# Transposing part of the softmax weights with VectorE and DMA instead of TensorE, in an attention and feed-forward kernel

## The chip, the cores and the metric

The kernel runs on one core of one Trainium2 chip. The metric is the device time in microseconds (us) of one execution. Of the kernel before there are three runs: 1382.41, 1383.41 and 1386.02 us, median 1383.41 us.

## The reference

Attention over 4 batches of 8 heads, with queries averaged in neighbouring pairs, followed by two feed-forward layers.

```python
batch, n_heads, seq, head_dim = (4, 8, 1152, 64)
q_pool = q.reshape(B, H, S // 2, 2, D).mean(axis=3)          # 576 queries per head
scores = scale * np.matmul(q_pool, k.transpose(0, 1, 3, 2))
scores = scores - np.max(scores, axis=-1, keepdims=True)
attn = np.exp(scores)
attn = attn / (np.sum(attn, axis=-1, keepdims=True) + 1e-09)
x = np.matmul(attn, v)                       # heads side by side: (2304, 512)
h = x @ w_in;  x = np.maximum(0.01 * h, h) @ w_out            # d_ff 2048
h = x @ w_in2; out = np.where(h > 0, h, np.exp(np.minimum(h, 0)) - 1) @ w_out2
```

All inputs are float32 except the four weight matrices, which arrive as float64.

## The kernel before

Precision. TensorE works on a reduced float32 type (F32R). Every operand that matters is split in two: a high part, rounded to F32R by a copy, and a low part, which is the value less the high part. `psplit` (L342) emits the two: the copy, mostly on ScalarE ("ACT"), and the subtraction on VectorE ("DVE") or GpSimd ("POOL"). The weights arrive as float64, and `convert` (L356) turns them into float32 bit by bit on ScalarE, VectorE and GpSimd.

Attention. A head pair (`attn_pair`, L631) is two heads of a batch; there are 16, in order. For each head the keys are transposed to `kT`, the queries summed in pairs, transposed and split to `qT`, the values split to `vn`. A pair has nine query tiles of 128 rows: four per head, and a ninth that holds the last 64 queries of both heads. For each tile `scores` (L517) works in three thirds of 384 keys: two matmuls per third into a PSUM bank (L531), the maximum on VectorE (L536, L538), and the exponential on ScalarE (L542), which leaves the third of P, the unnormalised softmax weights, as `p` in SBUF, with queries in partitions and keys along the row. P times V needs the keys in partitions, so `transpose_p` (L548) lets TensorE transpose three 128x128 blocks per third into a PSUM bank (L554), ScalarE copies the bank to the high part of `pt` (L345) and VectorE subtracts for the low part (L352). `pt` is one buffer per third for a group of two tiles (256 queries; 320 where the ninth tile joins). `pv` (L568) runs six matmuls per third and group (L578), then adds the two partial results into `xu` (L592).

Feed-forward. `mlp` (L676) runs a layer for one batch: for each of 16 slices of 128 hidden columns an up-projection (L721) with its activation and split, and for every four slices a down-projection (L755). `load_w` (L390) brings a slice's weights: the first time it loads, converts and splits them and writes both parts to DRAM; afterwards it loads the split parts, two transfers of 256 KB per matrix and slice, one for each part.

Order. Nothing runs in the order of the code. Every operation is entered with `prog.add` under an engine, a cost in nanoseconds and a rank; `Program.schedule` (L101) plays the program through with these costs and, whenever an engine is free, starts the ready operation of the lowest rank. `LATENCY` gives the delay from the end of an operation to its users; `HOLD`, `GAP`, `PATIENCE` and the bank caps are its further rules. The order so found is the order in each engine's queue. A pair has nine ranks; `PLAN` gives each batch and layer of the feed-forward its first rank and its span, so that its matmuls fill TensorE beside the attention of later pairs. All DMAs are issued by SyncE ("SP"), in one queue in that order, and wait there for their data. Buffers of a tag are used in rotation: an operation that first writes a buffer waits for the readers of the one `bufs` places before.

## Time and profile before

| | |
|---|---|
| profiled execution, whole | 1383.44 us |
| its span, first to last instruction | 1381.6 us |
| TensorE busy | 1346.1 us (97%) |
| ScalarE, VectorE, GpSimd busy | 903.0, 833.0, 523.7 us |
| DMA engines, mean share of the hardware queue | 43.5% |
| chain that ended last: TensorE, ScalarE, VectorE | 72%, 13%, 8% |

Times are microseconds from the span's start unless marked ns. "PE" is TensorE's matmul unit, "PEld" its weight load, which runs beside it. A matmul's busy time overlaps that of its neighbours, so the pace of TensorE is read from one start to the next and not from durations. The DMA share is the mean busy share of the core's 16 DMA engines. The time splits into three stages: to about 535 us the first nine pairs run beside the conversion of the weights and, later in it, the first feed-forward layers; from 535 to 1100 us the last seven pairs run beside the feed-forward of batches 1 and 2; after 1100 us only batch 3's feed-forward is left.

### The profile page before, as it was taken

The page shows a single profiled execution, that of the slowest core. Times are in us where ns is not written, and L with a number is a line of the kernel's source. Part 1 is how long each engine was busy: PE and PEld are TensorE (multiplying, and loading weights), DVE is VectorE, ACT ScalarE, POOL GpSimd, SP SyncE. Part 2 cuts the span into 40 slices and gives each one's busy share as a digit, 9 for nine tenths or more (in the row PEclk, how much of TensorE's full clock was granted, in tenths as well). Part 3 has the DMA queues.
Part 4 walks back from the last instruction along what each step waited for, and adds up shares of the span by engine and source line. Part 5 has one row for each costly group of instructions (what it writes and reads, how often), then busy time and mean ns, then how long its engine had stood idle before and what let it go on. Part 6 is the DMA issues. An engine that isn't in the chain of part 4 may idle for free.

```text
span 1381.6 us, 22560 instructions
## 1 busy us (share of the span) xinstructions
PE 1346.1 (97%) x7664; PEld 1161.1 (84%) x7664; DVE 833.0 (60%) x1919; ACT 903.0 (65%) x2391; POOL 523.7 (38%) x492
## 2 busy tenths in 40 slices
PE   7998999999999999999999999999999999999998
PEld 6887888888788888888888888888888888888887
DVE  6899997888888975455555555556555421232122
ACT  8999999898999976654666666564665333214331
POOL 4334466677767742221313132131311222223221
PEclk9999999999999999999999999999999999999999
DMA  4323446656566565433333444343443343333321
GB/s 139 113 88 98 156 146 211 217 197 212 188 215 219 192 214 169 144 132 131 116 119 129 137 164 147 122 164 115 147 137 139 136 168 122 123 107 137 122 77 46
DMA packets 119475, 202.29 MB, mean 146 GB/s; under 512 B 12608, under 2 KB 31040, under 8 KB 119360
## 3 DMA queue, kind: packets, MB, share of 16 engines
q1 hardware_dynamic: 119360, 200.85, 43.5%
q8 instruction: 61, 1.00, 0.3%
q14 instruction: 54, 0.44, 0.1%
HBM read 162.53 MB, written 38.27 MB: 145 GB/s over the span
## 4 chain that ended last, share of the span: by engine, by line
PE 72%; ACT 13%; DVE 8%; DMA 3%; POOL 2%; issue 2%; SPq 0%; ACTq 0%; POOLq 0%
PE b L755 26%; PE b L721 24%; PE b L578 7%; PE b L531 7%; PE b L554 6%; ACT p L542 4%; ACT pt L345 3%; DVE m L536 2%; DMA cr<-in_moe_w_out_dram 2%; DVE pt L352 2%; ACT cm L375 1%; ACT ct L377 1%; DVE wr L384 1%; PE b L485 1%; PE b L457 1%
## 5 line engine op out<-in xcount | busy, mean ns | idle before, releaser
L721 PE MATMUL b<-xs,wi 128*128 128x512 f32 x1440 | 404.0, 402 | 2.5 <-POOL xs L352 0.8
L721 PEld LDWEIGHTS b<-xs,wi 128*128 128x128 f32 x1440 | 256.2, 189 | 47.2 <-ACT p L542 1.1
L352 DVE TENSOR_TENSOR pt<-b,pt 128x384 fp32r<-128x384 f32 (+1 forms) x480 | 233.7, 511 | 90.4 <-ACT pt L345 87.5
L352 POOL TENSOR_TENSOR g<-t,g 128x512 fp32r<-128x512 f32 x112 | 144.8, 1294 | 364.6 <-ACT g L345 257.4
L542 ACT ACTIVATE p<-b,m 128x384 f32<-128x384 f32 x432 | 253.3, 600 | 24.8 <-DVE m L538 24.0
L345 ACT ACTIVATE pt<-b 128x384 fp32r<-128x384 f32 (+1 forms) x480 | 208.1, 470 | 82.0 <-PE b L554 81.0
L536 DVE TENSOR_REDUCE m<-b 128x1 f32<-128x384 f32 x432 | 230.3, 550 | 51.6 <-PE b L531 47.3
L554 PE MATMUL b<-ident,p 128*128 128x128 f32 x1296 | 200.3, 274 | 5.8 <-DVE pt L352 1.4
L755 PE MATMUL b<-g,wo 128*128 128x512 f32 x696 | 200.7, 403 | 0.0
L755 PE MATMUL b<-wo,g 128*128 128x512 f32 x696 | 198.8, 403 | 0.7 <-DVE t L739 0.7
L531 PE MATMUL b<-kT,qT 128*128 128x384 f32 x768 | 192.6, 352 | 5.5 <-DVE pt L352 2.6
L554 PEld LDWEIGHTS b<-ident,p 128*128 128x128 f32 x1296 | 159.9, 141 | 42.8 <-DVE pt L352 4.0
L578 PE MATMUL b<-pt,vn 128*128 128x256 f32 (+1 forms) x1152 | 191.0, 300 | 3.7 <-DVE pt L352 1.7
L578 PEld LDWEIGHTS b<-pt,vn 128*128 128x128 f32 x1152 | 169.4, 188 | 17.7 <-DVE pt L352 6.2
L531 PEld LDWEIGHTS b<-kT,qT 128*128 128x128 f32 x768 | 131.8, 191 | 21.3 <-DVE pt L352 3.5
L755 PEld LDWEIGHTS b<-wo,g 128*128 128x128 f32 x696 | 123.3, 188 | 20.5 <-DVE t L739 1.2
L755 PEld LDWEIGHTS b<-g,wo 128*128 128x128 f32 x696 | 121.9, 188 | 17.1
L382 POOL TENSOR_TENSOR wr<-wr,ct 128x256 uint32<-128x256 uint32 x128 | 92.4, 737 | 58.1 <-DVE wr L379 26.3
L769 DVE TENSOR_TENSOR acc<-b,acc 128x512 f32<-128x512 f32 x96 | 65.9, 687 | 72.3 <-PE b L755 71.0
L345 ACT ACTIVATE g<-t 128x512 fp32r<-128x512 f32 x112 | 71.2, 638 | 42.0 <-DVE t L732 24.9
L730 ACT ACTIVATE t<-b 128x512 f32<-128x512 f32 (+1 forms) x65 | 37.6, 584 | 93.1 <-PE b L721 92.1
L732 DVE TENSOR_TENSOR t<-b,t 128x512 f32<-128x512 f32 (+1 forms) x65 | 43.0, 663 | 89.7 <-ACT t L730 89.4
(117 smaller groups left out, 1694.5 us busy)
## 6 DMA issues: line engine op xcount, KB each, us to landing
wi<-w SPq DMA_DIRECT2D x176, 256.0 KB, 3.7
wo<-w SPq DMA_DIRECT2D x176, 256.0 KB, 3.8
cr<-in_moe_w_in_dram SPq DMA_DIRECT2D x64, 256.0 KB, 2.8
cr<-in_moe_w_out_dram SPq DMA_DIRECT2D x64, 256.0 KB, 3.2
w<-wi SPq DMA_DIRECT2D x64, 256.0 KB, 3.4
w<-wo SPq DMA_DIRECT2D x64, 256.0 KB, 3.4
raw<-in_k_dram SPq DMA_DIRECT2D x32, 288.0 KB, 3.7
raw<-in_v_dram SPq DMA_DIRECT2D x32, 288.0 KB, 3.4
```

The lines of the kernel that those rows point to most:

```text
L345: prog.add("ACT", act(n, sbuf=not psum), rank, lambda: A.activation(out=hi(), in_=src(), func=ACTF.Copy), w=[w], r=r)
L352: lambda: eng.tensor_tensor(out=lo(), in0=src(), in1=f32(hi()), op=ALU.subtract),
L382: prog.add("POOL", pool(CW), rank, lambda t=t, to=to: G.tensor_tensor(out=to(), in0=to(), in1=t.ap, op=ALU.add), w=part, r=[t] + part)
L531: PE.matmul(out=st[:, 0:384], lhsT=qa(a), rhs=kT[:, 384 * c:384 * c + 384], start=(i == 0), stop=(i == len(seq) - 1))
L536: prog.add("DVE", dve(384), rank - LR, lambda st=st, c=c: V.tensor_reduce(out=m[:, c:c + 1], in_=st[:, 0:384], axis=AX.X, op=ALU.max), w=[ ...
L542: prog.add("ACT", act(384, True), rank - LE, lambda c=c: A.activation(out=p[c].ap, in_=banks[c][:, 0:384], func=ACTF.Exp, bias=m[:, 3:4], ...
L554: PE.transpose(out=t[:, i, :], in_=p[c][:, 128 * i:128 * i + 128], identity=ident)
L578: PE.matmul(out=o[:, 0:n], lhsT=vn[:, c, :], rhs=pt[th][:, a, c % 3, :], start=(c == 3 * ORDER[0] and a == 0), stop=(c == 3 * ORDER[2] + 2 ...
L721: PE.matmul(out=h[:, 0:n], lhsT=wi[:, a, c, :], rhs=xs[hf][c][:, e], start=(c == 0 and a == 0 and e == 0), stop=(c == DC - 1 and a == 1))
L732: prog.add("DVE", dve(n), rk, lambda tn=tn, hn=hn: V.tensor_tensor(out=tn(), in0=hn(), in1=tn(), op=ALU.max), w=[t], r=[h, t])
L755: PE.matmul(out=y[:, 0:n], lhsT=g[f][hf][:, e, part] if layer else w[f][1][:, a, part], rhs=w[f][1][:, a] if layer else g[f][hf][:, e], st ...
L769: prog.add("DVE", dve(n), rank - HURRY, lambda y=y, a_=a_, n=n: V.tensor_tensor(out=a_.ap, in0=y[:, 0:n], in1=a_.ap, op=ALU.add), w=[a_], ...
```

## The change

For the last seven head pairs (`DTB = 9`: pairs 9 to 15) the eight full tiles of a pair no longer go through TensorE. `split_p` emits, per tile and third, one VectorE instruction that transposes 32x32 blocks of `p` within SBUF into half of a buffer of tag `wr` (two buffers; the tag of the raw weights, which come first in its rotation). When both tiles of a group are there, four DMAs, one for each 32 partitions, write the buffer to DRAM in runs of 768 bytes, and one DMA reads it back in runs of 3072 bytes into the low half of `pt`, now with keys in partitions. ScalarE copies these 768 columns to the high part and GpSimd subtracts for the low part. The ninth tile stays with TensorE. `pt` of these pairs has another column order (64 queries by three key blocks), which `pv` and the addition into `xu` undo.

The scheduler: a DMA is a `Move` with a cost for its issue and a time for which it occupies the DMA engines, one transfer after another; a DMA's result counts as landed at the end of that, plus 3000 ns instead of 2600. Buffers are linked when all operations are known (`link`), with `late` ones behind. Weights move as one transfer of 512 KB instead of two of 256 KB, and the raw form of a slice's two matrices shares one buffer. `PLAN`'s ranks are others.

```diff
+class Move(float):
+    def __new__(cls, runs, size, cost=420):
+        m = float.__new__(cls, cost)
+        m.serve = runs * (6 + 0.0456 * size) / 16
+        return m
...
-    LATENCY = {"PE": 200, "SP": 2600, "DVE": 130, "DVE POOL": 200, "ACT": 155, "ACT POOL": 170, "POOL": 150,
+    LATENCY = {"PE": 200, "SP": 3000, "DVE": 130, "DVE POOL": 200, "ACT": 155, "ACT POOL": 170, "POOL": 150,
...
+                    landed = end
+                    if e == "SP":
+                        landed = dma = max(dma, now + 300) + ops[i][1].serve
...
-                        t = end + self.latency(e, e2) if done else now
+                        t = landed + self.latency(e, e2) if done else now
...
-    WRB = 4
+    WRB = 2
...
-    PLAN = ((0, 0, 36, 21, 0), (0, 1, 57, 21, 0), (1, 0, 78, 16.5, 0), (1, 1, 94.5, 16.5, 0),
+    PLAN = ((0, 0, 36, 23, 0), (0, 1, 59, 23, 0), (1, 0, 82, 17.8, 0), (1, 1, 99.8, 17.8, 0),
...
+    DTB = 9
+    DTC = (0, 1, 2)
+    DTE = ("POOL", "POOL", "POOL")
+    DTR = 0
+    DTL = 1
...
         for i, w in enumerate((wi, wo)):
             if (layer, f, i) in kept:
                 kp = kept[layer, f, i]
-                for a in range(2):
-                    prog.add("SP", 400, rank - WAHEAD, lambda i=i, a=a, kp=kp: nc.sync.dma_start(
-                        out=f32(flat[i](a)), in_=kp[:, a]), w=[(w, a)], r=[kp])
+                prog.add("SP", Move(128, 4096), rank - WAHEAD, lambda w=w, kp=kp: nc.sync.dma_start(
+                    out=f32(both(w)), in_=kp.ap), w=[w], r=[kp])
...
-    def transpose_p(rank, p, dests):
-        for c in ORDER:
+    def by_dma(b, hp):
+        return b * NP + hp >= DTB
+
+    def split_p(rank, b, hp, j, g, half, p, pt, c0):
+
+        cs = DTC if by_dma(b, hp) else ()
+        transpose_p(rank, p, [(pt, c0, 0, 128)], [c for c in ORDER if c not in cs], by_dma(b, hp))
+        for c in cs:
+            if not half:
+                turned[j, g, c] = sb("wr", [128, 4, 3, 2, 32], F32, WRB, 1)
+            tb = turned[j, g, c]
+            prog.add("DVE", dve(384) + 60, rank, lambda c=c, tb=tb: V.transpose(
+                out=tb[:, :, :, half, :].rearrange("p j k q -> p k j q"), in_=p[c].ap), w=[(tb, half)], r=[p[c]])
+        if not half:
+            return
+        for c in cs:
+            tb = turned[j, g, c]
+            d = Buf(lambda c=c: dram.tile([4, 32, 4, 192], F32, name=f"p{b}_{hp}_{j}_{g}_{c}"))
+            for i in range(4):
+                prog.add("SP", Move(128, 768, 600), rank + DTR, lambda d=d, i=i, tb=tb: nc.sync.dma_start(
+                    out=d.ap.rearrange("j a i r -> i a j r")[i],
+                    in_=tb[32 * i:32 * i + 32].rearrange("a j k t q -> a j (k t q)")), w=[(d, i)], r=[tb])
+            prog.add("SP", Move(128, 3072), rank + DTR, lambda c=c, d=d: nc.sync.dma_start(
+                out=f32(pt[c][:, 1, 0:4]).rearrange("p i k r -> p (i k r)"),
+                in_=d.ap.rearrange("j a i r -> (j a) (i r)")), w=[(pt[c], "d")], r=[d])
+            psplit(rank + DTL, "ACT", DTE[c], lambda c=c: pt[c][:, 0, 0:4], lambda c=c: pt[c][:, 1, 0:4],
+                   lambda c=c: f32(pt[c][:, 1, 0:4]), 3 * 256, (pt[c], ("h", 0)),
+                   [(pt[c], "d")], (pt[c], ("l", 0)), fast=False)
...
-    def new_pt(n):
-        pt = {c: sb("pt", [128, 2, 3, n], F32R, PTB) for c in ORDER}
+    def new_pt(n, mixed):
+        pt = {c: sb("pt", [128, 2, n // 64, 3, 64] if mixed else [128, 2, 3, n], F32R, PTB) for c in ORDER}
...
-                        out=o[:, 0:n], lhsT=vn[:, c, :], rhs=pt[th][:, a, c % 3, :],
+                        out=o[:, 0:n], lhsT=vn[:, c, :], rhs=pt[th][:, a, :, c % 3, :] if by_dma(b, hp) else pt[th][:, a, c % 3, :],
...
-            transpose_p(at, p, [(pts[j, g], c0, 0, 128)])
+            split_p(at, b, hp, j, g, int(c0 > 0), p, pts[j, g], c0)
```

How the queues stand now is shown at pair 13, the second of batch 3. First TensorE, before: the first tile of that pair. `p` are thirds of P, `wo` and `g` belong to the down-projection of a feed-forward layer, `kT` and `qT` to scores.

```order
L755 MATMUL b2_11705<-g_11253,wo_11062 128x512 [waits PE_49]
L755 MATMUL b2_11705<-g_11253,wo_11062 128x512 x2
L554 MATMUL b1_11710<-ident_58,p_11510 128x128 [waits Activation_49]
L554 MATMUL b1_11710<-ident_58,p_11510 128x128 x2
L554 MATMUL b6_11718<-ident_58,p_11521 128x128 [waits Activation_49]
L554 MATMUL b6_11718<-ident_58,p_11521 128x128 x2
L755 MATMUL b2_11705<-g_11437,wo_11085 128x512 x3
L554 MATMUL b4_11738<-ident_58,p_11532 128x128 [waits DVE_49]
L554 MATMUL b4_11738<-ident_58,p_11532 128x128 x2
L755 MATMUL b2_11705<-g_11463,wo_11378 128x512 x3
```

TensorE in the same pair now, where thirds of its first group meet V (`pt`, `vn`):

```order
L642 MATMUL b5_11340<-pt_11280,vn_10858 128x256
L642 MATMUL b5_11340<-pt_11280,vn_10858 128x256 [waits DMAHW2_49,Pool_49]
L642 MATMUL b5_11340<-pt_11280,vn_10858 128x256 x4
L825 MATMUL b7_11468<-wo_10796,g_10983 128x512 [waits Activation_49]
L825 MATMUL b7_11468<-wo_10796,g_10983 128x512 x2
L642 MATMUL b5_11340<-pt_11349,vn_10858 128x256 [waits Activation_49]
L642 MATMUL b5_11340<-pt_11349,vn_10858 128x256 [waits DMAHW7_49,Pool_49]
L642 MATMUL b5_11340<-pt_11349,vn_10858 128x256 x4
L825 MATMUL b7_11468<-wo_10886,g_11221 128x512 x3
L559 MATMUL b4_11496<-kT_11046,qT_11110 128x384 x2
L825 MATMUL b7_11468<-wo_11132,g_11324 128x512 x3
L559 MATMUL b2_11509<-kT_11046,qT_11110 128x384 [waits DVE_49,PE_49]
```

The triples of L554 are gone from these tiles, and the second of six P x V matmuls waits for GpSimd and a DMA where it waited for VectorE. Next VectorE, before, at the start of pair 13: maxima (`m`) and the low parts of `pt`.

```order
L538 TENSOR_REDUCE m_11695<-m_11695 128x1 [waits DVE_49]
L352 TENSOR_TENSOR pt_11725<-b1_11710,pt_11725 128x3x128 [waits Activation_49]
L352 TENSOR_TENSOR pt_11732<-b6_11718,pt_11732 128x3x128 [waits Activation_49]
L536 TENSOR_REDUCE m_11758<-b7_11748 128x1 [waits PE_49]
L352 TENSOR_TENSOR pt_11751<-b4_11738,pt_11751 128x3x128 [waits Activation_49]
L536 TENSOR_REDUCE m_11758<-b1_11761 128x1 [waits PE_49]
L536 TENSOR_REDUCE m_11758<-b0_11766 128x1 [waits PE_49]
```

VectorE now, in the second group of pair 13:

```order
L587 STREAM_TRANSPOSE wr_11391<-p_11253 128x3x4x32 [waits DMAHW5_49,DMAHW7_49,DMAHW1_49,DMAHW0_49]
L564 TENSOR_REDUCE m_11401<-b7_11376 128x1 [waits PE_49]
L564 TENSOR_REDUCE m_11401<-b4_11386 128x1 [waits PE_49]
L564 TENSOR_REDUCE m_11401<-b1_11396 128x1 [waits PE_49]
L587 STREAM_TRANSPOSE wr_11282<-p_11374 128x3x4x32 [waits Activation_49]
L566 TENSOR_REDUCE m_11401<-m_11401 128x1 [waits DVE_49]
L374 TENSOR_TENSOR xs_11384<-xu_9787,xs_11384 128x512
L587 STREAM_TRANSPOSE wr_11391<-p_11382 128x3x4x32 [waits Activation_49]
```

Where VectorE subtracted, it now transposes blocks; the first transpose into a buffer waits for four DMAs, those that write its former content to DRAM, and the maxima of the next scores stand behind it. Last SyncE's queue, now, at the same group (`p3_1_..` are the pieces of P in DRAM, `wi` and `w0` weights):

```order
L595 DMA p3_1_0_1_0_11423<-wr_11282 32x4x192 [waits DMAHW2_49,DVE_49]
L595 DMA p3_1_0_1_0_11423<-wr_11282 32x4x192 [waits DMAHW3_49]
L595 DMA p3_1_0_1_0_11423<-wr_11282 32x4x192 [waits DMAHW4_49]
L595 DMA p3_1_0_1_0_11423<-wr_11282 32x4x192 [waits DMAHW5_49]
L595 DMA p3_1_0_1_1_11449<-wr_11391 32x4x192 [waits DMAHW6_49,DVE_49]
L426 DMA wi_11457<-w0_4_0_2919 128x1024 [waits DMAHW7_49,PE_49]
L595 DMA p3_1_0_1_1_11449<-wr_11391 32x4x192 [waits DMAHW0_49]
L595 DMA p3_1_0_1_1_11449<-wr_11391 32x4x192 [waits DMAHW1_49]
L595 DMA p3_1_0_1_1_11449<-wr_11391 32x4x192 [waits DMAHW2_49]
L855 DMA out_0_dram<-acc_10204 128x512 [waits DMAHW3_49,DVE_49]
L598 DMA pt_11490<-p3_1_0_1_0_11423 128x768 [waits DMAHW5_49,DMAHW4_49]
```

Before, this queue held in this stage only loads of weights, keys, queries and values and stores of the output; now the writes and reads of P stand between them, and a read waits at the head until its four writes have landed.

## Rows read from the trace of the kernel before

**Rows 1.** busy time, share of the span and instructions of each engine (page, part 1):
```profile
span 1381.6 us, 22560 instructions
...
PE 1346.1 (97%) x7664; PEld 1161.1 (84%) x7664; DVE 833.0 (60%) x1919; ACT 903.0 (65%) x2391; POOL 523.7 (38%) x492
```

**Rows 2.** stages: length; busy us of PE, PEld, DVE, ACT, POOL; clock; DMA share, GB/s:
```profile
0.00:535.00 535.00, 506.38 (x3059) 438.32 (x3060) 449.84 (x1104) 489.46 (x1373) 313.67 (x312) 1.00 0.53 172
535.00:1100.00 565.00, 563.61 (x3142) 486.70 (x3142) 313.63 (x692) 331.35 (x845) 138.99 (x110) 1.00 0.41 140
1100.00:1382.00 282.00, 276.15 (x1466) 236.07 (x1464) 69.55 (x124) 82.20 (x174) 71.05 (x70) 1.00 0.33 111
```

**Rows 3.** what TensorE waited for, 535 to 1100 us: us, times, longest:
```profile
PE b L554 <- ACT kT L470: 0.9, 1, 0.9
PE b L721 <- DVE acc L769: 0.2, 1, 0.2
```

**Rows 4.** timeline of TensorE: start us, us, engine, line, operation, out<-in, count:
```profile
1003.73 2.25 PE L755 MATMUL b<-wo,g 128*128 128x512 f32 x9
1005.82 0.49 PE L554 MATMUL b<-ident,p 128*128 128x128 f32 x3
1006.07 0.94 PE L755 MATMUL b<-wo,g 128*128 128x512 f32 x3
1006.84 0.49 PE L554 MATMUL b<-ident,p 128*128 128x128 f32 x3
...
1009.25 0.87 PE L578 MATMUL b<-pt,vn 128*128 128x256 f32 x6
1009.96 0.52 PE L531 MATMUL b<-kT,qT 128*128 128x384 f32 x2
1010.32 0.87 PE L578 MATMUL b<-pt,vn 128*128 128x256 f32 x6
```

**Rows 5.** groups by shape: line engine op out<-in xcount | busy us, mean ns | idle before, releaser:
```profile
L542 ACT ACTIVATE p<-b,m 128x384 f32<-128x384 f32 x432 | 253.3, 600 | 24.8 <-DVE m L538 24.0
...
L352 DVE TENSOR_TENSOR pt<-b,pt 128x384 fp32r<-128x384 f32 x384 | 204.4, 551 | 67.1 <-ACT pt L345 64.7
...
L345 ACT ACTIVATE pt<-b 128x384 fp32r<-128x384 f32 x384 | 182.1, 501 | 54.5 <-PE b L554 53.6
...
L379 DVE TENSOR_SCALAR wr<-cm 128x256 uint32<-128x256 uint32 x128 | 47.7, 395 | 3.7 <-ACT cm L375 3.1
L352 POOL TENSOR_TENSOR kn<-raw,kn 128x576 fp32r<-128x576 f32 x32 | 45.7, 1429 | 17.4 <-ACT kn L345 10.8 <-DVE wr L384 3.0 <-issue 1.0
...
L739 DVE SCALAR_TENSOR_TENSOR t<-t,b 128x512 f32<-128x512 f32 x59 | 40.3, 685 | 71.1 <-ACT t L737 69.4 <-ACT xu L345 1.0
...
L345 ACT ACTIVATE kn<-raw 128x576 fp32r<-128x576 f32 x32 | 22.9, 717 | 1.6 <-DMA raw<-in_k_dram 1.6
```

**Rows 6.** DMA, 535 to 1100 us: queue's packets, MB, share; issues, KB, us to landing:
```profile
q1 hardware_dynamic: 43047, 78.39, 41.0%
...
wi<-w SPq DMA_DIRECT2D x126, 256.0 KB, 3.4
...
raw<-in_k_dram SPq DMA_DIRECT2D x10, 288.0 KB, 4.1
...
qrem<-in_q_dram SPq DMA_DIRECT2D x6, 32.0 KB, 3.2
```

**Rows 7.** timeline of SyncE's queue: start us, us, line, out<-in, count:
```profile
726.81 0.86 SPq L401 DMA_DIRECT2D wo<-w  x2
729.39 5.18 SPq L401 DMA_DIRECT2D wi<-w  x4
```

**Rows 8.** DMA issues of 1100 to 1382 us:
```profile
out_dram<-acc SPq DMA_DIRECT2D x8, 256.0 KB, 2.2
out_dram<-cr SPq DMA_DIRECT2D x4, 128.0 KB, 2.3
```

**Rows 9.** the stage with the busiest DMA engines, columns as in rows 2:
```profile
400.00:450.00 50.00, 48.60 (x262) 40.58 (x261) 39.32 (x96) 47.94 (x132) 36.28 (x37) 1.00 0.69 225
```

More of the change, by code (lines that the diff above doesn't have):

```diff
@@ L52, in __init__, with buf, link @@
         self.ops, self.tags, self.psum, self.row = [], {}, [], {}
-    def buf(self, tag, bufs, make):
-        used = self.tags.setdefault(tag, [])
-        b = Buf(make, used[-bufs] if len(used) >= bufs else None, used[-1] if used else None)
-        used.append(b)
-        return b
+    def buf(self, tag, bufs, make, late=0):
+        b = Buf(make)
+        self.tags.setdefault(tag, []).append((late, bufs, b))
+        return b
+    def link(self):
+        for used in self.tags.values():
+            used.sort(key=lambda x: x[0])
+            for i, (_, bufs, b) in enumerate(used):
+                b.prev = used[i - bufs][2] if i >= bufs else None
+                b.before = used[i - 1][2] if i else None
     def bank(self, use, cap, make):
@@ L70, in add @@
         me = len(self.ops)
-        deps, starts, frees, allocs = set(), set(), [b.prev for b in want if b.prev is not None], []
+        deps, starts, frees, allocs = set(), set(), list(want), []
         def hits(accesses, part):
@@ L87, in add @@
                     allocs.append(b)
-            if b.prev is not None:
-                frees.append(b.prev)
-            if b.before is not None:
-                starts.add(b.before)
+            frees.append(b)
+            starts.add(b)
             b.writers.append((me, part))
@@ L101, in schedule @@
     def schedule(self):
+        self.link()
         ops, n = self.ops, len(self.ops)
@@ L107, in schedule @@
             for b in frees:
-                d.update(o for o, _ in b.writers + b.readers)
+                if b.prev is not None:
+                    d.update(o for o, _ in b.prev.writers + b.prev.readers)
             d.discard(i)
-            starts = {b.first for b in starts}
+            starts = {b.before.first for b in starts if b.before is not None} - {i}
             for o in d:
@@ L136, in schedule @@
         times = [0.0]
-        port = 0.0
+        port = dma = 0.0
         left = n
@@ L321, with sb @@
     prog = Program()
-    def sb(tag, shape, dt=F32, bufs=1):
-        return prog.buf(tag, bufs, lambda: sp.tile(shape, dt, tag=tag, name=tag, bufs=bufs))
+    def sb(tag, shape, dt=F32, bufs=1, late=0):
+        return prog.buf(tag, bufs, lambda: sp.tile(shape, dt, tag=tag, name=tag, bufs=bufs), late)
     def bank(use, shape, dt=F32, when=1):
@@ L361, in convert, with load @@
             g = sb("cm", [128, CW], F32, CB)
-            part = [(dst, n)]
-            def load(n=n, r=r):
+            part = [(dst, o + n)]
+            kn = CW // src.shape[2] if len(src.shape) == 3 else 1
+            def load(n=n, r=r, kn=kn):
                 rv = r.ap.rearrange("p n t -> p (n t)")
                 if len(src.shape) == 3:
-                    k0, kn = n // src.shape[2], CW // src.shape[2]
+                    k0 = n // src.shape[2]
                     rv, sv = rv.rearrange("p (c n) -> p c n", c=kn), src[:, k0:k0 + kn, :]
@@ L428, with load @@
     xr = [sb(f"xr{hp}", [128, RQ * B], F32) for hp in range(NP)]
-    def load(rank, key, tag, shape, pieces, bufs):
+    def load(rank, key, tag, shape, pieces, bufs, rows=128):
         t = sb(tag, shape, F32, bufs)
         for i, (to, src) in enumerate(pieces):
-            prog.add("SP", 400, rank, lambda to=to, src=src: nc.sync.dma_start(out=to(t), in_=src), w=[(t, i)])
+            prog.add("SP", Move(rows, 2304 if rows == 128 else 512), rank, lambda to=to, src=src: nc.sync.dma_start(out=to(t), in_=src), w=[(t, i)])
         raw[key] = t
@@ L449, in load_rem @@
              [(lambda t, j=j: t[64 * j:64 * j + 64],
-               q[b, 2 * hp + j, 256 * QT:S].rearrange("(p r) d -> p r d", r=2)) for j in range(2)], 2)
+               q[b, 2 * hp + j, 256 * QT:S].rearrange("(p r) d -> p r d", r=2)) for j in range(2)], 2, 64)
     def tr_r(rank, src, get, n, want):
@@ L546, in scores, with transpose_p @@
         return p
-    def transpose_p(rank, p, dests):
-        for c in ORDER:
+    def by_dma(b, hp):
[24 more added lines that the diff above has]
+                   [(pt[c], "d")], (pt[c], ("l", 0)), fast=False)
+    def transpose_p(rank, p, dests, order=ORDER, mixed=False):
+        for c in order:
             t = pbank("t")
@@ L591, in pv @@
         for to, c0, o0, k in pieces:
-            prog.add("DVE", dve(k), rank + PVLAG, lambda to=to, c0=c0, o0=o0, k=k: V.tensor_tensor(
-                out=to[hi, c0:c0 + k], in0=o[hi, o0:o0 + k], in1=tm[hi, o0:o0 + k], op=ALU.add),
+            mixed = to is x and by_dma(b, hp)
+            order = lambda ap, t, i, mixed=mixed: ap.rearrange(
+                f"p ({t} {i} q) -> p i t q", t=2, i=4) if mixed else ap
+            prog.add("DVE", dve(k), rank + PVLAG, lambda to=to, c0=c0, o0=o0, k=k, order=order: V.tensor_tensor(
+                out=order(to[hi, c0:c0 + k], "t", "i"), in0=order(o[hi, o0:o0 + k], "i", "t"),
+                in1=order(tm[hi, o0:o0 + k], "i", "t"), op=ALU.add),
                 w=[(to, (j, c0))], r=[o, tm])
@@ L629, in normalise @@
                 op=ALU.mult), w=[(xr[hp], (j, RQ * b))], r=[t2])
+    turned = {}
     def attn_pair(at, b, hp, nxt):
@@ L639, in tile_ @@
             if new:
-                pts[j, g] = new_pt(new)
-            transpose_p(at, p, [(pts[j, g], c0, 0, 128)])
+                pts[j, g] = new_pt(new, by_dma(b, hp))
+            split_p(at, b, hp, j, g, int(c0 > 0), p, pts[j, g], c0)
         if nxt:
```

52 lines of the change are left out of this document (32 added, 20 removed).

## Prediction

> **What bounds the kernel now.** I read the busy times first, then the same times by stage, then what TensorE waited for, then its timeline. TensorE is busy 97% of the span and no other engine more than 65% [rows 1]. By stage that share is uneven [rows 2]. Up to 535 us (head pairs 0 to 8, the first feed-forward layers and the weights' conversion) ScalarE is busy 489.46 of 535 us and TensorE 506.38. From 535 to 1100 us, where the last seven pairs run, TensorE is busy 563.61 of 565 us, while VectorE has 313.63, ScalarE 331.35, GpSimd 138.99 and the DMA engines a share of 0.41. TensorE waited 1.1 us in that whole stage [rows 3], at a granted clock of 1.00. So the stage that the change rebuilds is bound by TensorE's own instructions: what leaves its queue there is worth its full price, as long as nothing that replaces it makes TensorE wait.
>
> **What is removed.** Each of seven pairs has 8 full query tiles with 3 thirds of P each; a third was three TensorE transposes: 7 x 8 x 3 = 168 triples, 504 instructions. (The ninth tile of a pair keeps its triples.) The price is read between starts [rows 4]: a triple at 1005.82 and the next matmul at 1006.07 is 0.25 us. The three 512-column matmuls behind it take 0.77 us to the next start (1006.07 to 1006.84), while nine in a row take 2.09 us (1003.73 to 1005.82), 0.70 per three. A triple set between matmuls thus costs 0.25 + 0.07 = 0.32 us: 168 x 0.32 = 54 us. Where triples stand side by side the 0.07 falls once, so 168 x 0.25 = 42 us is the lower end; I take 54, as in most places of this stage a triple stands alone. With the triples go 168 ScalarE copies of 384 columns at 501 ns (84 us) and 168 VectorE subtractions at 551 ns (93 us) [rows 5].
>
> **What is added, on engines with room.**
> - VectorE: 168 block transposes of 128x384, SBUF to SBUF. No row shows one. The nearest is the 384-column subtraction at 551 ns; the ends are the 256-column SBUF instruction at 395 ns and the 512-column one at 685 ns [rows 5]. At 0.55 us VectorE stays as it is; the ends are -26 and +23 us of VectorE, in a stage where it has 251 us free.
> - ScalarE: 84 copies of 768 columns. 576 columns take 717 ns; at the same per column 0.96 us: 80 us, against 84 removed. Nothing.
> - GpSimd: 84 subtractions of 768 columns. 576 columns take 1429 ns; at the same per column 1.91 us each, 160 us: from 139 to some 299 of about 511 us. (Both of these rows in [rows 5].)
> - DMA: 336 writes of 98,304 bytes and 84 reads of 393,216, 66.1 MB. In this stage 78.39 MB took 41.0% of 565 us [rows 6], 2.96 us per MB, so 195 us more: 427 of about 511 us, a share of 0.84. The merging of the weight transfers leaves their bytes as they are.
> - SyncE: 420 issues more, and in this stage about 130 fewer from the merged weights. One issue took 0.43 us, and 1.3 each in the burst of four at 729.39 [rows 7]. At 0.4 us some 590 issues are 236 us of 511.
> - P x V reads its moving operand in pieces of 64 columns. Its six matmuls stand 0.71 us apart now (1009.25 to 1009.96); the ends are nothing and, if they went like 384-column ones (0.36 per two), 504 x 0.06 = 30 us. I take nothing, as columns and bytes are the same.
>
> **The new waits.** Until now a third went from scores through TensorE, ScalarE and VectorE. Now it goes: VectorE's maximum (0.55, as its subtraction) and up to three exponentials at 0.60 [rows 5], block transpose 0.55, four issues 1.6, landing 3.2 (the smallest transfer of the stage, 32 KB [rows 6]), read issue and landing 0.4 + 4.1, ScalarE 0.96, GpSimd 1.91: 15.5 us. In the new order I counted the TensorE work between a third's last score matmul and its P x V matmuls, with the paces of rows 4: 17.9 us at the least of 84 thirds, 28 at the median. That covers the chain, so P x V need not wait while transfers land as in rows 6.
> The tighter place is VectorE. Two buffers hold the turned thirds, and the first block transpose into one waits until the four writes out of it have landed; behind it on VectorE stand the score maxima (so the exponentials, so TensorE's score banks) and the feed-forward's activation. Between the last transpose into a buffer and the next use of it VectorE has 1.9 to 9.9 us of instructions, about 5 at the median, priced by rows 5; it is idle 44% of the stage, so this distance is some 1.6 times as long on the clock. The writes need 1.6 + 3.2 = 4.8 us: only the 8 of 82 distances under 3.0 us fall short, by 0.7 us on average. I charge 6 us for these and 4 for reads at SyncE's head that hold the transfers behind them: 10 us on TensorE. The bounds are 0 and the third rival's 62.
> The rest of the program (the other order in the first 535 us, whole weights instead of halves, other feed-forward spans) I set at nothing. TensorE idles 28.6 us there and 5.9 at the end [rows 2]; the same work in another order may move this by 6 us either way, ScalarE being its cover and its limit.
>
> **Sum.** The profiled execution took 1383.44 us, 1381.6 of them span; the median of the runs is 1383.41, so no correction. 1383.4 - 54 + 10 = 1339.4, told as 1340. With 42 instead of 54 it is 1351, without waits 1329: the forecast's own range is 1327 to 1355.
>
> **Rivals.**
> 1. *The DMA engines become the bound.* They have 33 us of work per pair now (0.41 x 565 / 7) and get 28 more: 61 us in the 73 us that TensorE then needs. Half of the added bytes leave SBUF from 32 partitions at a time. If these go at half the pace, 14 us more make 75 us. For it: in the last stage 128 KB out of 64 partitions landed in 2.3 us and 256 KB out of 128 in 2.2 [rows 8], no sooner with half the bytes. Against it: 32 KB landed no sooner than 128 [rows 6], so these times may be latency. The stretch with the busiest DMA engines, 0.69, lost TensorE 1.4 of 50 us [rows 9]; with that much lost on top of 75, a pair takes 77.2 us against today's 80.7 (565 / 7): 1383.4 - 7 x 3.5 = 1359 us. The Trainium skill states such a rule (SBUF — State Buffer, "Door 1: The DMA port swizzle"): a transfer's bandwidth depends on how many of 16 ports its partitions reach, and 32 or 64 partitions reach only 8. The two rows of the trace agree with it, and it would give the price above; without it the writes keep the pace of rows 6.
> 2. *The gain does not reach the end.* The last stage's 282 us depend on batch 3's feed-forward alone; if the attention ends sooner but its weights or inputs do not, the time stays about 1383. Against it: in the new order 37 triples of feed-forward matmuls of batch 2, 26 us at 0.70, still stand behind the last P x V, and TensorE has only 5.9 us idle there now.
> 3. *Writes land late and VectorE holds everything* (slower). A merged weight load is 512 KB, 1.55 us of all engines; two ahead of a write make its 4.8 us 7.9. Then the 36 of 82 distances with under 4.9 us of VectorE work fall short by 1.7 us on average: 62 us, more than the 54 won: 1383.4 - 54 + 62 = 1391. It decides once the writes need more than about 7.6 us. For it: SyncE issues in order, and writes stand between such loads. Against it: loads in this stage landed in 3.4 us at the median, and VectorE's wait reaches TensorE only after the score banks are used up.
>
> **How the numbers follow.** Forecast 0.71, first rival 0.13, second 0.05, third 0.11. The range takes in the first rival and the larger end of the gain: 1322 to 1380. A measurement of this kernel tells about 0.3% (4 us) from no change: faster 0.84, same 0.05, slower 0.11.
>
> **What would show it.** Right: in the stage of the last seven pairs TensorE is still busy over 97%, with three transposes per third of the ninth tile alone; a pair takes about 74 us; the block transposes take 0.5 to 0.6 us; VectorE's waits on writes stay under 30 us in sum; the DMA share is about 0.85. Wrong: TensorE's waits on GpSimd's halves of P or on score maxima reach tens of microseconds (rivals 1 and 3, told apart by whether the write's landing or the DMA share grew), or the stage gets shorter and the last one longer by as much (rival 2).

## The result and the profile after

The changed kernel takes 1327.65 us (median, 1326.54 to 1330.19) against 1382.91 us before in the same job: a ratio of 0.9599, 95% interval 0.9579 to 0.9619, 55.3 us faster. The profiled execution took 1330.2 us, 1328.4 of them span.

The busy times of the kernel after answer to [rows 1]:

```profile
span 1328.4 us, 22070 instructions
...
PE 1293.4 (97%) x7160; PEld 1115.7 (84%) x7160; DVE 839.4 (63%) x1919; ACT 895.5 (67%) x2307; POOL 677.7 (51%) x576
```

TensorE has 504 instructions fewer and 53 us less to do, ScalarE 84 instructions and 8 us less; GpSimd has 154 us more. The stages of the kernel after, with the columns of [rows 2]. The last seven pairs now end at 1050 us instead of 1100:

```profile
0.00:535.00 535.00, 507.17 (x3055) 442.10 (x3056) 459.53 (x1119) 490.98 (x1379) 318.09 (x315) 0.99 0.52 176
535.00:1050.00 515.00, 512.25 (x2663) 439.83 (x2662) 311.30 (x679) 322.75 (x756) 291.04 (x193) 1.00 0.84 278
1050.00:1328.00 278.00, 273.95 (x1445) 233.76 (x1445) 68.55 (x121) 81.77 (x173) 68.53 (x68) 1.00 0.32 112
```

The first stage is as it was, the last is 4 us shorter, and the stage of the seven pairs has gone from 565 to 515 us. TensorE is still busy 99% of it, the DMA engines' share has doubled to 0.84 and GpSimd's time too. What TensorE waited for from 535 to 1050 us, in the kernel after (answers to [rows 3]):

```profile
PE b L559 <- ACT p L570: 1.1, 3, 0.5
PE b L642 <- POOL pt L374: 0.9, 3, 0.4
PE b L791 <- DMA wi<-w: 0.6, 1, 0.6
PE b L791 <- POOL xs L374: 0.2, 1, 0.2
```

2.8 us in all. The new operations by shape, in the kernel after (columns as in [rows 5]): the copy and the subtraction of 768 columns, and the block transpose, which no row of before showed:

```profile
L374 POOL TENSOR_TENSOR pt<-pt 128x768 fp32r<-128x768 f32 x84 | 154.8, 1848 | 89.1 <-ACT pt L367 71.5 <-PE b L559 3.3 <-ACT rem L517 3.2
...
L587 DVE STREAM_TRANSPOSE wr<-p 128x384 f32<-128x384 f32 x168 | 92.1, 565 | 31.0 <-ACT p L570 17.2 <-DMA p<-wr 13.0
...
L367 ACT ACTIVATE pt<-pt 128x768 fp32r<-128x768 f32 x84 | 71.0, 846 | 16.0 <-DMA pt<-p 16.0
```

The DMA of 535 to 1050 us in the kernel after, with the columns of [rows 6]:

```profile
q1 hardware_dynamic: 82286, 142.71, 83.2%
...
wo<-w SPq DMA_DIRECT2D x64, 512.0 KB, 5.1
...
pt<-p SPq DMA_DIRECT2D x80, 384.0 KB, 4.8
p<-wr SPq DMA_DIRECT2D x317, 96.0 KB, 4.1
```

And TensorE's timeline around 826 us in the kernel after (columns as in [rows 4]); the triples that are left belong to the ninth tile:

```profile
825.80 0.86 PE L791 MATMUL b<-xs,wi 128*128 128x512 f32 x3
826.50 0.49 PE L611 MATMUL b<-ident,p 128*128 128x128 f32 x3
826.74 0.94 PE L791 MATMUL b<-xs,wi 128*128 128x512 f32 x3
827.52 0.52 PE L559 MATMUL b<-kT,qT 128*128 128x384 f32 x2
827.87 0.85 PE L791 MATMUL b<-xs,wi 128*128 128x512 f32 x3
828.56 1.04 PE L642 MATMUL b<-pt,vn 128*128 128x320 f32 x6
```

A triple is still 0.24 us between starts, and the three matmuls behind it take 0.78 us to the next start where the three behind a score matmul take 0.69.

To see where the 53 us went I added, over the whole trace of each kernel, the time from every matmul's start to the next one's start, by kind. Waits and a lower clock fall to the matmul in front of them, so the sums give the whole span but its ends:

| us, start to start | before | after | after with no pair by DMA (first experiment) |
|---|---|---|---|
| P's transposes (1296, 792, 1296 matmuls) | 133.1 | 89.1 | 134.2 |
| feed-forward, up and down (3743) | 837.2 | 824.6 | 832.0 |
| P x V (1152) | 161.9 | 162.4 | 161.4 |
| scores (960) | 183.6 | 189.3 | 187.9 |
| the other transposes (512) | 55.0 | 52.4 | 53.5 |

### The profile page after: what moved, and what is told of

Same layout as the page of the kernel before. It is cut to its first block, busy times and chain, and to the rows that moved or that the text cites. A ratio compares the mean times of both kernels' runs of the same rounds, so it can differ in the third digit from the quotient of the medians.

```text
span 1328.4 us, 22070 instructions
## 1 busy us (share of the span) xinstructions
PE 1293.4 (97%) x7160; PEld 1115.7 (84%) x7160; DVE 839.4 (63%) x1919; ACT 895.5 (67%) x2307; POOL 677.7 (51%) x576
## 2 busy tenths in 40 slices
DMA packets 143091, 268.33 MB, mean 202 GB/s; under 512 B 15232, under 2 KB 76672, under 8 KB 142976
## 4 chain that ended last, share of the span: by engine, by line
PE 80%; ACT 9%; DVE 6%; POOL 2%; issue 2%; DMA 1%; POOLq 0%; ACTq 0%; DVEq 0%
PE b L825 29%; PE b L791 27%; PE b L559 9%; PE b L642 9%; PE b L611 3%; ACT p L570 3%; ACT pt L367 2%; DVE m L564 2%; DVE pt L374 1%; PE b L485 1%; PE b L513 1%; ACT kT L498 1%; DVE wr L403 1%; ACT cm L399 1%; POOL pt L374 1%
## 5 line engine op out<-in xcount | busy, mean ns | idle before, releaser
L791 PEld LDWEIGHTS b<-xs,wi 128*128 128x128 f32 x1440 | 259.5, 189 | 50.9 <-POOL wi L374 4.1
L374 POOL TENSOR_TENSOR g<-t,g 128x512 fp32r<-128x512 f32 x112 | 145.0, 1296 | 139.5 <-ACT g L367 99.2
L374 POOL TENSOR_TENSOR pt<-pt 128x768 fp32r<-128x768 f32 x84 | 154.8, 1848 | 89.1 <-ACT pt L367 71.5
L825 PE MATMUL b<-g,wo 128*128 128x512 f32 x696 | 194.1, 400 | 0.0
L825 PE MATMUL b<-wo,g 128*128 128x512 f32 x696 | 187.6, 397 | 0.0
L374 DVE TENSOR_TENSOR pt<-b,pt 128x384 fp32r<-128x384 f32 (+1 forms) x312 | 143.8, 487 | 28.1 <-ACT pt L367 26.5
L825 PEld LDWEIGHTS b<-wo,g 128*128 128x128 f32 x696 | 127.3, 188 | 24.2
L367 ACT ACTIVATE pt<-b 128x384 fp32r<-128x384 f32 (+1 forms) x312 | 127.7, 455 | 25.6 <-PE b L611 24.7
L825 PEld LDWEIGHTS b<-g,wo 128*128 128x128 f32 x696 | 124.6, 188 | 20.2 <-issue 0.3
L611 PE MATMUL b<-ident,p 128*128 128x128 f32 x792 | 121.1, 274 | 4.0 <-DVE pt L374 2.0
L611 PEld LDWEIGHTS b<-ident,p 128*128 128x128 f32 x792 | 96.4, 141 | 23.2 <-DVE pt L374 2.7
L587 DVE STREAM_TRANSPOSE wr<-p 128x384 f32<-128x384 f32 x168 | 92.1, 565 | 31.0 <-ACT p L570 17.2
```

Of the source, the lines that this page charges most:

```text
L367: prog.add("ACT", act(n, sbuf=not psum), rank, lambda: A.activation(out=hi(), in_=src(), func=ACTF.Copy), w=[w], r=r)
L374: lambda: eng.tensor_tensor(out=lo(), in0=src(), in1=f32(hi()), op=ALU.subtract),
L587: prog.add("DVE", dve(384) + 60, rank, lambda c=c, tb=tb: V.transpose(out=tb[:, :, :, half, :].rearrange("p j k q -> p k j q"), in_=p[c].a ...
L611: PE.transpose(out=t[:, i, :], in_=p[c][:, 128 * i:128 * i + 128], identity=ident)
L791: PE.matmul(out=h[:, 0:n], lhsT=wi[:, a, c, :], rhs=xs[hf][c][:, e], start=(c == 0 and a == 0 and e == 0), stop=(c == DC - 1 and a == 1))
L825: PE.matmul(out=y[:, 0:n], lhsT=g[f][hf][:, e, part] if layer else w[f][1][:, a, part], rhs=w[f][1][:, a] if layer else g[f][hf][:, e], st ...
```

## The experiments

**Without the transposition by DMA.** All of the change but its main part:

```diff
-    DTB = 9
+    DTB = 16
```

> No pair is turned by VectorE and DMA; every other part of the change (whole-weight transfers, two wide weight buffers, the scheduler's dearer transfers, the new spans of the feed-forward layers) stays. Theory: the gain is the 168 triples of TensorE transposes alone, 0.26 us each for the triple between starts and about 0.075 us for the matmul behind it, as the two traces show (transposes 133.1 to 89.1 us, feed-forward matmuls 837 to 825): 1327.7 + 168 x 0.335 = 1384 us, between 1376 and 1392, TensorE's feed-forward matmuls back at 837 us. Rival: the order and the merged transfers gave 10 us or more of the gain by themselves: below 1374 us.

Measured: 1382.24 us, a ratio to before of 0.9986 (0.9977 to 0.9996). By themselves the other parts are worth about 2 us (0.5 to 3.2 by the interval). Transposes are back at 134.2 us and the feed-forward matmuls at 832.0, not all the way to 837: of the 12.6 us that they lost between the two kernels, 7.4 go with the triples and some 5 with the new order. Its row for 535 to 1100 us is that of [rows 2] again:

```profile
535.00:1100.00 565.00, 563.11 (x3126) 486.39 (x3124) 309.69 (x681) 324.47 (x826) 141.32 (x112) 1.00 0.41 142
```

**Four pairs by DMA.** `DTB = 12`.

> The last four pairs are turned by DMA instead of the last seven: 96 triples leave TensorE's queue, 72 come back. Theory: each triple has the same price wherever it stands in this stage: 1327.7 + 72 x 0.335 = 1352 us, between 1346 and 1358, and the DMA share of the stage falls with the number of pairs. Rival: with seven pairs something else than TensorE already holds a part (DMA engines or VectorE's buffers), so that the last three pairs won less than their share: 1345 us or less.

Measured: 1350.62 us (ratio 0.9756, 0.9742 to 0.9771). From none to four pairs 31.6 us for 96 triples, 0.33 each; from four to seven 23.0 for 72, 0.32 each. The price of a triple does not fall with the number of pairs, so at seven pairs I see no sign that anything but TensorE holds the stage.

**How transfers are counted.** The scheduler's two new counts, one at a time and together:

```diff
 # no_queue_3000; old_counting with "SP": 2600, no_queue_5000 with "SP": 5000 as well
-                        landed = dma = max(dma, now + 300) + ops[i][1].serve
+                        landed = end
 # queue_3800, alone
-    LATENCY = {"PE": 200, "SP": 3000, ...
+    LATENCY = {"PE": 200, "SP": 3800, ...
```

> The scheduler counts a transfer as before the change: landed 2.6 us after its issue, without a shared queue of the transfers ahead of it. All else as in the kernel after. Theory: TensorE's work bounds the stage and the distance from scores to P x V stays well over the chain of a third, so the counting is worth little: 1328 within 8 us. Rival: the dearer counting is what keeps TensorE from waiting, and without it the thirds arrive late at P x V: over 1345 us, with TensorE's waits on GpSimd's halves of P of 10 us or more.

> Of the two parts of the dearer counting only one is undone: the scheduler again takes every transfer as if it had the DMA engines to itself, but keeps 3.0 us from issue to landing. Theory (the count of the transfers ahead is what matters, since the DMA engines are 0.84 busy and a landing here takes from 1.5 to 7.8 us): the thirds come late at P x V again, 1370 to 1410 us. Rival (the 0.4 us of latency is what matters): 1328 within 8.

> No queue of transfers in the scheduler's count, but 5.0 us from issue to landing for every transfer, near the upper end of what the writes take in the kernel after (nine in ten land within 5.1 us of the issue's end). Theory (what matters is that P x V is set far enough behind its transfers, however that is counted): 1328 to 1345 us. Rival (only a count of the load places them well, a flat one moves the weights' and inputs' transfers as well and buys nothing): over 1360 us.

> The counting of the kernel after, made more pessimistic still: 3.8 us instead of 3.0 behind the queue of transfers. Theory: TensorE waits 2.8 us in the stage, so there is nothing left to win: 1328 within 5 us. Rival: with later P x V the buffers of P and V are held longer and the scheduler runs out of work to put between: 1335 us or more.

Measured: 1398.75 us with the old count (ratio 1.0113, 1.0096 to 1.0130), 1393.99 without the queue (1.0111, 1.0059 to 1.0161), 1366.23 without it at 5 us (0.9871, 0.9845 to 0.9897), 1357.97 with it at 3.8 us (0.9817, 0.9802 to 0.9832). My theory on the first fell, and so did those on the flat 5 us and on 3.8 us; that on the count without the queue held. With the old count the same transposition is 16 us slower than the kernel before, clear of the interval. It is the queue in the count that is worth this, 66 us, and not the 0.4 us, which is worth 5 us without the queue. Without the transposition the new count gave at most the 2 us or so of the first experiment. Each kernel's row from the first to the last start of a P x V matmul of the seven pairs (columns as in [rows 2]), the kernel after first:

```profile
531.00:1017.00 486.00, 483.46 (x2525) 416.21 (x2524) 301.58 (x664) 312.69 (x739) 282.70 (x187) 1.00 0.86 285
```

with the old count:

```profile
528.00:1078.00 550.00, 505.83 (x2517) 426.80 (x2517) 307.88 (x674) 314.89 (x744) 283.12 (x187) 0.97 0.77 251
```

without the queue at 5.0 us:

```profile
549.00:1050.00 501.00, 491.29 (x2542) 420.07 (x2541) 308.03 (x673) 316.49 (x745) 281.88 (x185) 1.00 0.84 276
```

and with the queue at 3.8 us:

```profile
557.00:1046.00 489.00, 483.99 (x2525) 415.97 (x2524) 301.80 (x662) 311.23 (x737) 282.84 (x186) 1.00 0.86 283
```

With the old count the seven pairs take 64 us more for the same matmuls: 44 us of TensorE idle instead of 2.5, and 22 us more busy at a mean granted clock of 0.97. What TensorE waited for most there, 528 to 1078 us, is the two halves of P that P x V reads, the sign that the rival named:

```profile
PE b L642 <- POOL pt L374: 18.4, 15, 3.6
PE b L642 <- ACT pt L367: 9.3, 6, 2.9
```

One such stall can be followed. TensorE in the kernel with the old count (start, length, what it stood idle for):

```profile
604.28 0.28 PE L642 MATMUL b<-pt,vn 128*128 128x256 f32 x1
608.15 1.02 PE L642 MATMUL b<-pt,vn 128*128 128x256 f32 x5 [3.59 <-POOL pt L374]
```

The read, ScalarE's copy and GpSimd's work of that third:

```profile
595.30 0.32 SPq L598 DMA_DIRECT2D pt<-p  x1
...
602.41 0.85 ACT L367 ACTIVATE pt<-pt 128x768 fp32r<-128x768 f32 x1 [4.43 <-DMA pt<-p]
...
603.83 1.28 POOL L507 TENSOR_TENSOR qn<-raw 128x512 f32<-128x512 f32 x1 [4.96 <-PE b L642]
605.07 1.26 POOL L374 TENSOR_TENSOR g<-t,g 128x512 fp32r<-128x512 f32 x1
606.29 1.80 POOL L374 TENSOR_TENSOR pt<-pt 128x768 fp32r<-128x768 f32 x1
```

VectorE at the same place:

```profile
595.35 0.58 DVE L587 STREAM_TRANSPOSE wr<-p 128x384 f32<-128x384 f32 x1 [4.20 <-DMA p<-wr]
...
604.12 1.04 DVE L587 STREAM_TRANSPOSE wr<-p 128x384 f32<-128x384 f32 x2 [5.35 <-DMA wo<-w]
```

and the same stretch by windows:

```profile
600.00:604.00 4.00, 4.00 (x25) 3.56 (x25) 0.00 (x0) 1.59 (x3) 0.17 (x1) 1.00 1.01 385
604.00:608.00 4.00, 0.56 (x4) 0.30 (x2) 1.61 (x3) 0.75 (x2) 4.00 (x3) 1.00 1.02 384
609.00:612.00 3.00, 3.00 (x11) 2.90 (x11) 0.71 (x2) 1.85 (x3) 1.67 (x1) 0.50 0.81 261
```

Here the DMA engines are full (1.01, 1.02), though over the seven pairs they are less busy (0.77) than in the kernel after (0.86). The read issued at 595.30 lets ScalarE start only at 602.41, some 7 us later, where reads in the kernel after land in 4.8 us at the median. GpSimd then has two other instructions in front of this third's subtraction, which starts at 606.29. TensorE stops for 3.6 us, and after that its clock is granted at half, 1.2 GHz, for the three microseconds from 609. VectorE's idle time from 600 to 604 us is a wait for writes too (the last of the four that it needs lands at 604.0), but it cannot be the cause of this stop: what it transposes at 604.12 belongs to later thirds, since the read of this one was issued at 595.30.

What the count changes shows in the order. I priced the matmuls between a third's last score matmul and its first P x V matmul, each at the median time of its shape from start to start. This distance is 18.0 us at the least and 28.3 at the median in the kernel after, 16.3 and 24.0 with the old count, 16.5 and 24.7 without the queue, 20.2 and 27.7 without it at 5.0 us, and 20.1 and 30.0 with it at 3.8 us. The two kernels that are slower than before are the two with the short distance. Their transfers land no later: at the median a write takes 3.5 us with the old count and 3.6 without the queue, and 4.0 over the whole of the kernel after. So the queue in the count sets P x V further behind its scores; that it also spreads the transfers is not shown.

More caution does not help. At 3.8 us the seven pairs take nearly the same time (489 us) but begin 26 us later; at 5.0 us without the queue they begin 18 us later and take 15 us more. The last converted weight is written at 537.3 and 537.1 us instead of 507.7 (the last start of L408 in each trace). I take the reason to be that every load of the conversion is counted as late as well and that the turned thirds take over the conversion's buffers; no run separates this.

**More transfers.** Each write a second time into DRAM that nobody reads, or one extra copy of the turned third; the extra issues cost the scheduler nothing, so all orders stay:

```diff
+            for i in range(4):        # each_write_twice
+                prog.add("SP", Move(0, 0, 1), ..., out=d2...[i], in_=tb[32 * i:32 * i + 32]...)
+            prog.add("SP", Move(0, 0, 1), ..., out=d2.ap, in_=tb...)   # one_copy_beside
```

> Each write of a turned third is issued a second time, into another DRAM tile that nobody reads: 336 more issues and 33 MB more, all engines' orders unchanged. Theory: at 2.96 us per MB this is 98 us more of the DMA engines' time, 433 + 98 = 531 of 515 us: the DMA engines become the bound, the stage grows by at least 16 us, TensorE waits on weights and on GpSimd's halves of P for some 20 to 40 us: 1345 to 1370 us. Rival: the engines' busy share overstates their load (a queue's latency counts as busy), so there is room: the share rises by less than 0.1 and the time stays at 1328 within 6. Second rival: VectorE, whose buffers wait for twice as many writes, holds everything: more than 1370 us with over 100 us of VectorE's waits on writes.

> The same 33 MB more as in the run with each write issued twice, but as one transfer of 384 KB per third in runs of 3072 bytes, out of all 128 partitions: 84 more issues at SyncE instead of 336. All engines' orders are unchanged. Theory (the DMA engines' time is what ran out): 10752 packets at the 141 ns that this kernel's 3072-byte reads took are 95 us per engine, nearly the 112 us that the doubled writes added, so nearly the same loss: 1410 to 1445 us. Rival (SyncE's issues ran out, four more of them ahead of each read, or VectorE's two buffers that wait for eight landings): with one issue more of 0.35 us per third most of the loss goes: 1332 to 1365 us.

Measured: 1440.71 us (ratio 1.0405, 1.0385 to 1.0425) and 1367.08 us (0.9886, 0.9868 to 0.9905). The same 33 MB cost 113 us in 336 issues and 39 us in 84. So the theory of both runs, the DMA engines' time alone, fails; the doubled writes show both signs of their second rival (over 1370 us, over 100 us of VectorE's waits on writes), and the one copy lies 2 us above its rival's range. The queue's row and the waits tell it; the DMA of 535 to 1050 us with the one copy:

```profile
q1 hardware_dynamic: 92136, 167.62, 94.8%
```

and with each write twice, moving fewer bytes in the same time at a lower share:

```profile
q1 hardware_dynamic: 112826, 147.65, 90.8%
```

VectorE's waits on writes (us, times, longest), with each write twice, 535 to 1140 us:

```profile
DVE wr L587 <- DMA x<-wr: 73.3, 39, 4.9
DVE wr L587 <- DMA p<-wr: 49.7, 20, 5.3
```

and with the one copy, 535 to 1085 us:

```profile
DVE wr L587 <- DMA x<-wr: 56.3, 36, 4.2
DVE wr L587 <- DMA p<-wr: 25.5, 12, 4.7
```

VectorE waits 123 us on writes with each write twice, 82 with the one copy and 13 in the kernel after; TensorE waits on GpSimd's halves of P 28.6, 10.7 and 0.9 us. My reading is that four more issues of 0.45 us ahead of each read put every later transfer back and hold the buffers longer. The one copy costs 39 us at a share of 0.95, with one issue more per third. How much of either loss is SyncE's, how much VectorE's buffers' and how much the DMA engines' is not separated.

**Which way the writes are cut.** By column block instead of by partition block, same bytes, runs and count; then with a DRAM piece whose rows are numbered through (this one reads the third back with its rows in another order, so it leaves out putting P in the order that V needs; the work is the same):

```diff
-    out=d.ap.rearrange("j a i r -> i a j r")[i], in_=tb[32 * i:32 * i + 32]...
+    out=d.ap.rearrange("j a i r -> j i a r")[i], in_=tb[:, i]...      # writes_by_column_block
+    out=d.ap.rearrange("j a i r -> j (a i) r")[i], in_=tb[:, i]...    # rows_of_all_partitions
```

> The four writes of a third are cut by column block instead of by partition block: each leaves SBUF from 128 partitions with one run of 768 bytes each, instead of from 32 partitions with four runs each; bytes, runs, issues and the order are the same. Theory (a transfer's pace here is set by its bytes and runs): the writes land in 4.1 us as before within 0.4, the DMA share of the stage stays at 0.84, 1328 us within 4. Rival (32 partitions reach fewer ports and go at half the pace): the writes land 1 us or more sooner and the DMA share falls to 0.75 or less; the time stays at 1328 within 4 all the same, since TensorE waits only 2.8 us in the stage.

> As the writes by column block, but each write now goes to one contiguous piece of DRAM, so that its list of rows has 128 rows at its outermost step instead of 4 groups of 32 (the third is then read back with its rows in another order, so P is permuted: the number of transfers, bytes and runs stay). Theory: the 161 us that the writes by column block lost came from their outermost step of 4, by which only 4 of the 16 engines carried a write (12 fewer landing signals per write: packets under 512 bytes 15232 to 11200). With 128 rows outermost all 16 carry it: 1328 us within 5, packets under 512 bytes back at 15232. First rival: leaving SBUF a column block at a time is slow by itself: over 1400 us again. Second rival (32 partitions at a time go at half the pace): the writes land at least 0.6 us sooner than the 3.6 us after the issue's end that they take in the kernel after, and the DMA share falls from 0.84 to 0.78 or less, time 1328 within 5.

Measured: 1489.03 us (ratio 1.0753, 1.0735 to 1.0771), against both theory and rival; then 1327.08 us (0.9600, 0.9585 to 0.9614). The packets of the whole run by column block:

```profile
DMA packets 139059, 268.32 MB, mean 180 GB/s; under 512 B 11200, under 2 KB 72640, under 8 KB 138944
```

with rows of all partitions:

```profile
DMA packets 143091, 268.33 MB, mean 202 GB/s; under 512 B 15232, under 2 KB 76672, under 8 KB 142976
```

The data are the same; what is missing by column block is 4032 small packets, 12 for each of 336 writes. The 420 transfers that the kernel with no pair by DMA lacks go with 6720 such packets, 16 each (15232 less 8512), so I take them for the engines' signals of a landing: 4 of 16 engines signalled each write by column block. Its packets of 768 bytes were no slower (37 ns in the mean of the records, 40 in the kernel after). 43,008 of them on 4 engines are 43,008 x 37 ns / 4 = 398 us on each, on top of the other transfers' 433 - 109 = 324 us (0.84 of 515, less 43,008 x 40.5 ns / 16): 722 us by this estimate. That is 7% above the 675 us (535 to 1210) that the stage takes there, so it is too high, but it leaves these four engines no room, while the mean share of all 16 is 0.62. The packets' records agree: exactly four packets are under way during 169 of the 675 us and exactly sixteen during 134. VectorE's wait on the writes in that stage:

```profile
DVE wr L587 <- DMA p<-wr: 175.6, 57, 6.9
```

The Trainium skill states this as a rule (DMA: Bandwidth & Descriptors, "Why a DMA increments its semaphore by 16 and not by 1"): a transfer issued as here, by a hardware queue, takes as many engines, up to 16, as divide the slowest dimension of both its access patterns, and only those post a signal; the 12 missing packets per write and the time agree.

Against the rule of ports that the first rival rested on, rows of all partitions is the test: 128 partitions at a time instead of 32. The writes land in 4.0 instead of 4.1 us and the DMA share of 535 to 1050 us is 0.81 instead of 0.84:

```profile
q1 hardware_dynamic: 81655, 141.85, 80.8%
...
p<-wr SPq DMA_DIRECT2D x315, 96.0 KB, 4.0
```

A packet of 768 bytes takes 37 ns in the mean of the records instead of 40: a tenth, not a half. This is for four such writes issued one behind the other among other transfers; no run has one by itself.

**Weights in halves, and the old spans.**

```diff
+    for a in range(2): ... out=kp[:, 512 * a:512 * a + 512]   # weights_in_halves, stores and loads
-    PLAN = ((0, 0, 36, 23, 0), ... (2, 0, 117.6, 15.2, 0), ...
+    PLAN = ((0, 0, 36, 21, 0), ... (2, 0, 111, 16.5, 0), ...  # old_spans
```

> The prepared weights are stored and loaded in two halves of 256 KB again, as before the change; the order of all engines stays, with each second half right behind its first at SyncE. Theory: some 130 issues more in the stage at 0.36 us are 47 us of SyncE, from 242 to 289 of 515 us, and hide: 1328 within 5. Rival: SyncE holds the writes of turned thirds back behind them and VectorE waits for its buffers: VectorE's wait on writes grows from 13 to over 50 us and the time to 1340 or more.

> The feed-forward layers' places and spans of before the change (21, 21, 16.5, 16.5, 16.5, 16.5 instead of 23, 23, 17.8, 17.8, 15.2, 15.2 units), all else as in the kernel after. Theory: the spans only set which feed-forward matmuls fill which wait; TensorE's work is the same and the fillers suffice either way: 1328 within 10. Rival: the new spans are what gives the last seven pairs enough matmuls between scores and P x V, and without them the thirds come late: over 1345 us.

Measured: 1334.21 us (ratio 0.9650, 0.9635 to 0.9664) and 1337.86 us (0.9675, 0.9661 to 0.9689). They are some 7 and 10 us slower than the kernel after. The halves lie 1 us above their theory's range and below the rival; the old spans lie just inside their theory's range. What TensorE waited for with weights in halves, 535 to 1055 us:

```profile
PE b L648 <- POOL pt L374: 5.8, 8, 1.4
```

With the transposition by DMA the merged transfers are worth about 7 us, most of it in these waits (0.9 us in the kernel after). VectorE's waits on writes, the rival's sign, came to 17 us and not 50. The halves are more issues (SyncE's issues last 298 of 520 us, 238 of 515 in the kernel after) and also more packets, since each run of 4096 bytes became two; which of the two counts is not shown. With the old spans TensorE's waits of 535 to 1060 us come to 7.0 us in all, 4.1 of them on GpSimd's halves of P; the rest of the 10 us is not explained.

## Why the prediction was right, point by point

- *The bound.* TensorE bound the stage and still does: 512.25 of 515 us.
- *What is removed.* Forecast 54 us, 0.25 per triple and 0.07 for the matmuls behind. Measured between the two traces: 44.0 us on the triples (0.26 each) and 12.6 on feed-forward matmuls. The experiments with none, four and seven pairs give 0.32 to 0.33 us per triple on the clock, 54.6 us in all. Of the 12.6 us, some 5 came from the order, as the first experiment shows, and the scores' matmuls cost some 4 us more in that order (183.6 before, 187.9 there, 189.3 in the kernel after). So the feed-forward matmuls gave back 7.4 us for the 168 triples, 0.04 each where I had 0.07; the price of a triple was right in the sum and somewhat too high in this part.
- *What is added.* Block transpose 565 ns (0.55 forecast), ScalarE's copy 846 (960), GpSimd's subtraction 1848 (1910), DMA share 0.84 (0.84), GpSimd 291 us in the stage (299). SyncE's 577 issues from 530 to 1048 us last 242 us (236 for 590). P x V with pieces of 64 columns: 119 and 147 ns at the median from start to start for 256 and 320 columns after 535 us, against 118 and 147 in the kernel before, nothing lost.
- *P x V's wait.* It waited 0.9 us on GpSimd and for nothing else new. But the cover is thinner than I had it. From the end of the last block transpose ahead of a third's writes to the end of GpSimd's half took 16.6 us at the median (11.8 to 23.6), where the same terms of my chain are 12.2: writes land in 4.1 us instead of 3.2 and reads in 4.8 instead of 4.1, and the rest is time between the steps, which I had at nothing. (The terms of the whole chain, as printed, add up to 15.1 us and not to 15.5.) At the longest the chain exceeds the least cover of 17.9 us that I counted. P x V starts 1.1 us after that end at the median, and in 10 of 84 thirds within 0.3 us of it or before it.
- *The 10 us of waits: the step that failed.* I charged 6 us for VectorE's buffers and 4 for reads at SyncE's head. VectorE did wait on writes, 13.0 us in 13 places where I had 8 places and 6 us; none of it is found in TensorE's waits beyond the 1.1 us on exponentials above. I take it that score banks, and matmuls that stand ready, took it up; no run tests that. At 0 the sum is 1329, which I gave as the end without waits; the measured 1327.65 is 2 below it, and 12 below the 1340 of the forecast.
- *The first rival* had nothing to it at this load: writes from 32 partitions went at nine tenths of the pace of writes from 128. There is little room above this load, though: with the one copy, at a share of 0.95, the time is 1367 us.
- *The second rival*: the last stage went from 282 to 278 us; the gain reached the end.
- *The third rival* did not come, but it was the right one to fear, and the scheduler's count is what kept it away. Without the queue in the count the time is 1394 us where the rival's price was 1391, but that they meet is chance. VectorE's waits on writes from 528 to 1078 us are 30.5 us there, half of the rival's 62, and TensorE waited most at P x V on the two halves of P (13.1 us on GpSimd, 4.2 on ScalarE), which I had put at nothing because the order covered the chain. My working took this order as it stood and did not ask which part of the change made it hold.

## What to carry to other kernels

When work leaves a bound engine for the DMA engines, count the starts between instructions for what it wins, and let the planner see the queue of transfers: here the same transposition won 55 us with the queue counted and, without it, lost 11 us at the same latency. A flat allowance of 5 us for every transfer was no substitute here: it won 17 us. Mind the outermost dimension of a transfer: 4 cost 161 us here, while 32 and 128 cost nothing.

## What the runs showed of the hardware

- A block transpose of 128x384 values of 4 bytes, SBUF to SBUF, takes 565 ns on VectorE, as a 384-column subtraction does [rows 5].
- Writes whose outermost dimension was 4 left 4 instead of 16 small packets each, as if on 4 of 16 DMA engines, and cost 161 us; with 128 rows outermost, out of the same 128 partitions, the 161 us were back.
- After a stop of TensorE of 3.6 us its clock was granted at 1.2 GHz from 609 to 612 us; over the seven pairs with the old count the mean was 0.97, and TensorE was busy 22 us longer for the same matmuls. There a stall cost more than its length.
